# Two tiles of query features against the key-value sums at a time, in a fused attention and mixture-of-experts kernel

## The chip, the core and the metric

The kernel runs on one core of a Trainium2 chip. The metric is the device time of one execution in microseconds (us), the median of three runs. Engines are named as in the profile: PE (matrix multiplications; PEld are its weight loads), DVE (vector), ACT (activations), POOL (general purpose), SP (here it only issues DMAs).

## The reference

For 2048 tokens of width 512: layer norm, projections to queries, keys and values of 32 heads of 16, a feature map of each query and key (a small matrix per head, then two softmaxes of 16), and linear attention, whose numerator and denominator come from sums over all tokens.

```python
kv = jnp.einsum("bhsf,bhsd->bhfd", phi_k, v)
z  = jnp.einsum("bhsf->bhf", phi_k)
num = jnp.einsum("bhqf,bhfd->bhqd", phi_q, kv)
den = jnp.einsum("bhqf,bhf->bhq", phi_q, z)[..., None] + 1e-6
o = num / den
...
h = x + _A_ref(_layernorm(x, axis=-1), A_wqkv, A_w_phi, A_wo)
h2 = h + _B_ref(_layernorm(h, axis=-1), B_w_gate, B_w1, B_w2)
```

`_A_ref` ends with the output product `@ wo`. `_B_ref` sends each token to the one of eight experts with the largest logit; an expert is a product to 1792 columns, a silu, and a product back to 512.

## The kernel before

The 2048 tokens are 16 tiles of 128. The first 177 us make the projections, the sums over keys and values (`kvbd`, which holds each head's sums and its denominator column) and the turned query features `phT0` to `phT15`, one per tile. The change lies in the stage behind that, the **attention-output stage**, from 177 us to 257 us of the span. Behind it follow the experts, in pairs of tiles, until the end.

The stage is the loop `for c in range(NT + 8)` (L1034). For a tile it has these steps, each run at its own distance behind the loop's counter:

- `s_num(c)` (L511) starts a DMA of the input tile `xt` two tiles ahead, issues 32 small products `pn` (L523, weights of 128x64, 68 columns) into two PSUM banks, and lets DVE invert the denominators (L527 `den`) and multiply (L528 `o`).
- `s_ot(c-1)` turns `o` with four PE transposes `pto` (L480); ACT splits it into a high part `xh` (L84) and DVE into the rest `xl` (L87). In what follows `xh(c)` and `xl(c)` are those of tile c.
- `s_wo(c-2)` is the output product `po` (24 matmuls, L90 to L92, high and low parts of the weights `wohi`, `wolo`); DVE adds the input to give `hb` (L924, or L928 in halves) and the gate logits `lg`; ACT sums `hb` (L932) and sums its squares (L935), with the negative mean `hnm` (POOL, L934) between the two. Further POOL steps (L937 to L939) finish the layer norm.
- every second tile, for a pair of tiles, DVE picks the expert (`s_top`), POOL works out the gate (`s_gate`, L966 to L971) and SP writes the pair to `hbuf` in DRAM (L972); PE and DVE rank the tokens within their experts (`s_rank`, products `pl`; `s_inv`, products `acc`).
- after eight tiles `s_star` chooses the expert that will go first: product `pc` (L1011), then DVE steps to the register value `esti` (L1017). SP loads it (L276) and starts four DMAs of that expert's weights, `raw0` to `raw3` (L278). `s_first` finds which tokens go first (product `gp0`, L1028; DVE `gidx` and `sidx`, L1029 and L1030), and POOL gathers them into `xg0` (L168).
- from then on the weights are split: ACT makes `whi` out of `raw` in quarter pieces (L84), DVE makes `wlo` (L235). They stand on ACT and DVE between the last tiles' steps.

The stage ends with the turn `mtr` of the first gathered tokens (L197), the output product of tile 15, and the first expert's first product `mh` (256.76 us).

Each engine works through its own queue in order, and waits at the head of it for semaphores of the others. The order of a queue is made when the kernel is built, by a scheduler that follows the program's order and the `after(...)` constraints. PSUM has four banks that `pn`, `pto`, the tile's own `po` (tiles 0, 13 and 15), `mtr` and `mh` take in turn: who takes a bank waits until its last contents have been read. The other output products share one pair of banks. There are five buffers for `xt`.

Of the kernel before, what the change touches and what calls it, by code (L numbers as in the profile page):

```python
# [27 lines left out]
NT = S // P  # L28
# [27 lines left out]
def kernel(  # L56
# [20 lines left out]
    def bc(ap, n):  # L77
        return ap.unsqueeze(len(ap.shape)).to_broadcast(list(ap.shape) + [n])
# [29 lines left out]
    po, pol, isS, nS, mS, isP = [pos[:, i:i + 1] for i in range(6)]  # L108
# [38 lines left out]
    def after(i):  # L147
        return tc.issue_after(i.ins) if i is not None else ExitStack()

    def bank(name):  # L150
        return ps.tile([P, 512], F32, name=name, tag="b")
# [263 lines left out]
    with ExitStack() as actx:  # L415
# [40 lines left out]
        st = [dict() for _ in range(NT)]  # L456

        def row(name, bufs, tag):
            return work.tile([P, D], F32, name=name, tag=tag, bufs=bufs)

        def load_x(c, queue=nc.sync):
            st[c]["xt"] = row("xt", 5, "xt")
            queue.dma_start(st[c]["xt"], x[c * P:(c + 1) * P, :])
# [33 lines left out]
        def proj2(ab, whi, wlo, name, outer=False, own=False):  # L497
            pw = None
            if outer or own:
                p = [bank(name) for _ in range(2)]  # L500
            else:
                pw = psw.tile([P, 2, 512], F32, name=name, tag="w")
                p = [pw[:, i, :] for i in range(2)]
            for a in range(KD if outer else 2):
                for b in range(2 if outer else KD):
                    i, k = (b, a) if outer else (a, b)
                    m = mm3(p[i][:, 0:HC], ab[0][:, k, :], ab[1][:, k, :], whi[:, k, i, :], wlo[:, k, i, :],
                            k == 0, k == KD - 1)
            return p, m, pw

        def s_num(c):  # L511
            if c == 0:
                load_x(0)
                load_x(1)
            if c + 2 < NT:
                load_x(c + 2)
            o = row("o", 2, "pc").rearrange("p (h f) -> p h f", f=DH)
            for i in range(2):
                pn = bank("pn")
                for g in range(4):  # L520
                    for s in range(2):
                        r = slice(64 * s, 64 * s + 64)
                        st[c]["pn"] = T.matmul(pn[r, g * 68:(g + 1) * 68], phT[c][:, 4 * i + g, r],  # L523
                                               kvbd[:, 4 * i + g, :], start=True, stop=True)
                nv = pn[:, 0:272].rearrange("p (h f) -> p h f", f=DH + 1)
                den = work.tile([P, 16, 1], F32, name="den")
                V.reciprocal(den, nv[:, :, DH:DH + 1])  # L527
                st[c]["on"] = V.tensor_tensor(o[:, 16 * i:16 * i + 16, :], nv[:, :, 0:DH],  # L528
                                              den.to_broadcast([P, 16, DH]), op=OP.mult)
            st[c]["o"] = o.rearrange("p h f -> p (h f)")  # L530
# [5 lines left out]
        if True:  # L536
# [106 lines left out]
            def feat1(p, c, whole=True):  # L643
                pv = p.rearrange("p (h f) -> p h f", f=DH)
                mn = work.tile([P, H], F32, name="mn")
                V.tensor_reduce(mn, pv, AX.X, OP.min)
                t = wp.tile([P, H, 2, DH], F32, name="t", bufs=3)
                V.tensor_tensor(t[:, :, 1, :], bc(mn, DH), pv, op=OP.subtract)
                return feat1b(p, c, t) if whole else t

            def feat1b(p, c, t):
                pv = p.rearrange("p (h f) -> p h f", f=DH)
                mx = work.tile([P, H], F32, name="mx")
                V.tensor_reduce(mx, pv, AX.X, OP.max)
                pin["f1"] = V.tensor_tensor(t[:, :, 0, :], pv, bc(mx, DH), op=OP.subtract)  # L655
                pin["ex"] = A.activation(t, t, AF.Exp, scale=st[c]["rstd"])  # L656
                return t.rearrange("p h s f -> p (h s) f")
# [244 lines left out]
                    pin["kv"] = V.tensor_tensor(kvbd[r, :, 17 * h:17 * h + 17], kvps[0][r, :, k:k + 17], epsz[r], op=OP.add)  # L902
            with after(pin["kv"]):
                t15 = feat1(pq[2], NT - 1, False)
            s_num(0)
            s_num(1)
            s_ot(0)

# [2 lines left out]

        def s_wo(c):
            b, j = divmod(c, NB)
            with after(st[min(c + 2, NT - 1)]["pn"]):
                p, st[c]["po"], po = proj2(st[c]["oT"], wohi, wolo, "po", own=c in (0, NT - 3, NT - 1))
            if j == 0:
                bt[b]["hb"] = work.tile([P, NB * ROW], F32, name="hb", tag="ph", bufs=3).rearrange(
                    "p (j r) -> p j r", r=ROW)
                bt[b]["lg"] = work.tile([P, NB, E], F32, name="lg", bufs=3)
            h = bt[b]["hb"][:, j, :]  # L920
            hv, xv = h[:, 0:D].rearrange("p (i d) -> p i d", i=2), st[c]["xt"].rearrange("p (i d) -> p i d", i=2)
            lg = bt[b]["lg"][:, j, :].rearrange("p (i e) -> p i e", i=2)
            if po is not None:
                V.tensor_tensor(hv, po[:, :, 0:D // 2], xv, op=OP.add)  # L924
                st[c]["lg"] = V.tensor_tensor(lg, po[:, :, D // 2:HC], xwg[:, c], op=OP.add)
            else:
                for i in range(2):
                    V.tensor_tensor(hv[:, i, :], p[i][:, 0:D // 2], xv[:, i, :], op=OP.add)  # L928
                    st[c]["lg"] = V.tensor_tensor(lg[:, i, :], p[i][:, D // 2:HC], xwg[:, c, i, :], op=OP.add)
            junk = row("junk", 3, "xn")  # L930
            sm = work.tile([P, 2], F32, name="hsum")
            A.activation(junk, h[:, 0:D], AF.Copy, accum_out=sm[:, 0:1])  # L932
            nm = work.tile([P, 1], F32, name="hnm")
            G.tensor_scalar(nm, sm[:, 0:1], -1.0 / D, None, op0=OP.mult)  # L934
            st[c]["sq"] = A.activation(junk, h[:, 0:D], AF.Square, bias=nm, accum_out=sm[:, 1:2])  # L935
            ve = work.tile([P, 1], F32, name="ve")
            G.tensor_scalar(ve, sm[:, 1:2], 1.0 / D, EPS, op0=OP.mult, op1=OP.add)  # L937
            G.tensor_tensor(h[:, D + 1:D + 2], ve, nhalf, op=OP.pow)
            st[c]["hp"] = G.tensor_tensor(h[:, D:D + 1], nm, h[:, D + 1:D + 2], op=OP.mult)  # L939
# [65 lines left out]
        def at(fn, c, n=NT):  # L1005
            if 0 <= c < n:
                fn(c)
# [25 lines left out]
        LOS = {NT - 4: range(0, 2), NT - 3: range(2, 4), NT - 2: range(4, 6), NT - 1: range(6, 8)}  # L1033
        for c in range(NT + 8):  # L1034
            if c > 1:
                at(s_num, c)
                if c == NT - 3:
                    s_wo(c - 2)
                at(s_ot, c - 1)
# [16 lines left out]
            if c not in (NT - 3, NT + 1):  # L1056
                at(s_wo, c - 2)
            if c in (4, 6, 8):
                s_qt(NT - 3 + c // 2 - 2)
            if c == NT:  # L1060
                with after(st[NT - 2]["po"]), after(st[NT - 1]["oT"][2]), after(st[NT - 2]["lg"]):
                    x0 = xhi[0][:, :, 0:P], xlo[0][:, :, 0:P]
                    xl0 = turn(*x0)[1]
                with after(pin["mtr"]):
                    s_wo(NT - 1)
                with after(st[NT - 1]["hp"]):
                    s_gate(b)
# [602 lines left out]
```

## Time and profile before

| | us |
|---|---|
| median of 3 runs (lowest, highest) | 633.71 (633.68, 633.88) |
| the profiled execution's own time | 634.18 |
| its span | 632.4 |
| attention-output stage in the span | 177.1 to 256.8 |
| ACT, busy over the span | 373.3 |
| POOL, busy over the span | 246.6 |

Start times below are us from the span's start. A row of the timeline has the start, the busy time, the engine, the line and the operation, the tiles written and read, the shape, the count of equal instructions joined in the row, and in square brackets the idle time ahead of it with what ended it. The duration of a PE row has a modelled end, so that neighbouring rows overlap; PE's pace is read from the distance of starts. The profiled execution took 0.47 us longer than the median.

### The profile page before, as it was taken

The page shows a single profiled execution, that of the slowest core. Times are in us where ns is not written, and L with a number is a line of the kernel's source. Part 1 is how long each engine was busy: PE and PEld are TensorE (multiplying, and loading weights), DVE is VectorE, ACT ScalarE, POOL GpSimd, SP SyncE. Part 2 cuts the span into 40 slices and gives each one's busy share as a digit, 9 for nine tenths or more (in the row PEclk, how much of TensorE's full clock was granted, in tenths as well). Part 3 has the DMA queues.
Part 4 walks back from the last instruction along what each step waited for, and adds up shares of the span by engine and source line. Part 5 has one row for each costly group of instructions (what it writes and reads, how often), then busy time and mean ns, then how long its engine had stood idle before and what let it go on. Part 6 is the DMA issues. An engine that isn't in the chain of part 4 may idle for free. (4 is left out here: it accounts for less than half of the span.)

```text
span 632.4 us, 14731 instructions
## 1 busy us (share of the span) xinstructions
PE 622.4 (98%) x5455; PEld 555.0 (88%) x5455; DVE 452.2 (72%) x900; ACT 373.3 (59%) x673; POOL 246.6 (39%) x345
## 2 busy tenths in 40 slices
PE   8999999999999999999999999999999999999996
PEld 7888888888889999868998899999999889988884
DVE  7988786888898788966324666666555775579992
ACT  6666766577434449634325666566456666668781
POOL 5586778787616554521122221210401420023220
PEclk9999999999999999999999999999999999999998
DMA  8712111111002359249221586563755595569921
GB/s 315 253 36 61 42 51 52 51 52 35 18 20 85 118 205 380 85 160 399 78 72 43 170 299 206 208 235 135 267 174 206 180 336 170 195 217 372 421 83 36
DMA packets 25689, 103.09 MB, mean 163 GB/s; under 512 B 3422, under 2 KB 3422, under 8 KB 17536
## 3 DMA queue, kind: packets, MB, share of 16 engines
q1 hardware_dynamic: 21088, 88.15, 39.1%
q0 software_dynamic: 4368, 13.82, 6.5%
q8 instruction: 46, 0.75, 0.5%
q14 instruction: 43, 0.35, 0.2%
q10 hardware_dynamic: 144, 0.02, 0.0%
HBM read 93.56 MB, written 8.81 MB: 162 GB/s over the span
## 5 line engine op out<-in xcount | busy, mean ns | idle before, releaser
L235 DVE TENSOR_TENSOR wlo<-raw,whi 128x1024 fp32r<-128x1024 f32 (+1 forms) x133 | 152.0, 1166 | 27.2 <-ACT whi L84 24.9
L84 ACT ACTIVATE whi<-raw 128x1024 fp32r<-128x1024 f32 (+1 forms) x134 | 129.1, 998 | 1.5 <-DVE wlo L235 0.6
L168 POOL DMA_INDIRECT xg<-hbuf,gidx x34 | 43.4, 1275 | 134.2 <-DMA out_dram<-xg,sidx 34.1
L87 DVE TENSOR_TENSOR hA<-hs,hA 128x256 fp32r<-128x256 f32 (+1 forms) x84 | 36.6, 435 | 74.7 <-ACT hA L84 53.7
L664 POOL TENSOR_TENSOR ph<-t,sm 128x1024 f32<-128x1024 f32 x32 | 62.1, 1941 | 16.9 <-DVE sm L662 16.6
L90 PE MATMUL gw<-xhi,whi 128*128 128x256 f32 x224 | 64.1, 286 | 0.0
L91 PE MATMUL gw<-xlo,whi 128*128 128x256 f32 x224 | 63.0, 281 | 0.0
L92 PE MATMUL gw<-xhi,wlo 128*128 128x256 f32 x224 | 63.0, 281 | 0.0
L1419 ACT ACTIVATE hs<-gw 128x256 f32<-128x256 f32 x56 | 21.4, 382 | 63.2 <-PE gw L92 52.7
L661 DVE TENSOR_REDUCE sm<-t 128x64 f32<-128x1024 f32 x32 | 38.9, 1215 | 20.0 <-ACT t L656 17.9
L656 ACT ACTIVATE t<-t,rstd 128x1024 f32<-128x1024 f32 x32 | 36.8, 1151 | 27.2 <-DVE t L655 24.7
L181 POOL DMA_INDIRECT out_dram<-xg,sidx x17 | 19.9, 1173 | 78.1 <-DVE xg L1271 42.9
L90 PEld LDWEIGHTS gw<-xhi,whi 128*128 128x128 f32 x224 | 42.2, 188 | 1.7
L91 PEld LDWEIGHTS gw<-xlo,whi 128*128 128x128 f32 x224 | 42.3, 189 | 1.6
L92 PEld LDWEIGHTS gw<-xhi,wlo 128*128 128x128 f32 x224 | 42.2, 189 | 0.0
L90 PE MATMUL po<-wohi,xh 128*128 128x260 f32 x128 | 37.4, 293 | 0.1
L84 ACT ACTIVATE hA<-hs 128x256 fp32r<-128x256 f32 (+1 forms) x84 | 35.8, 427 | 2.6
L92 PE MATMUL po<-wohi,xl 128*128 128x260 f32 x128 | 36.6, 286 | 0.3 <-DVE xl L87 0.2
L91 PE MATMUL po<-wolo,xh 128*128 128x260 f32 x128 | 36.1, 282 | 0.0
L90 PE MATMUL pv<-wvhi,xh 128*128 128x260 f32 x120 | 34.1, 284 | 0.0
L92 PE MATMUL pv<-wvhi,xl 128*128 128x260 f32 x120 | 33.9, 282 | 0.0
L91 PE MATMUL pv<-wvlo,xh 128*128 128x260 f32 x120 | 33.9, 282 | 0.0
(425 smaller groups left out, 1919.9 us busy)
## 6 DMA issues: line engine op xcount, KB each, us to landing
raw<-in_w_dram SPq DMA_DIRECT2D x63, 1024.0 KB, 6.5
xt<-in_x_dram SPq DMA_DIRECT2D x32, 256.0 KB, 2.7
hbuf<-hb SPq DMA_DIRECT2D x8, 515.0 KB, 3.6
xT<-in_xTs_dram SPq DMA_DIRECT2D x16, 256.0 KB, 2.6
phT<-in_wv_dram SPq DMA_DIRECT2D x4, 256.0 KB, 4.4
phT<-in_wqkT_dram SPq DMA_DIRECT2D x4, 256.0 KB, 5.1
phT<-in_wqkT_dram SPq DMA_DIRECT2D x2, 512.0 KB, 6.3
phT<-in_wo_dram SPq DMA_DIRECT2D x2, 512.0 KB, 8.2
```

Of the source, the lines that this page charges most:

```text
L84: return A.activation(dst, src, AF.Copy)
L87: return V.tensor_tensor(dst, src, hi.bitcast(F32), op=OP.subtract)
L90: T.matmul(ps, ahi, bhi, start=first, stop=False)
L91: T.matmul(ps, ahi, blo, start=False, stop=False)
L92: return T.matmul(ps, alo, bhi, start=False, stop=last)
L168: G.indirect_dma_start(out=dst[0:n, :], out_offset=None, in_=hbuf if col else hbuf[0:S // 2, :], in_offset=bass.IndirectOffsetOnAxis(ap=gi ...
L181: m = G.indirect_dma_start(out=out, out_offset=bass.IndirectOffsetOnAxis(ap=sidx[0:n, col:col + 1], axis=0), in_=src[0:n, 0:D], in_offset= ...
L235: return eng.tensor_tensor(lo, r, h.bitcast(F32), op=OP.subtract)
L656: pin["ex"] = A.activation(t, t, AF.Exp, scale=st[c]["rstd"])
L661: V.tensor_reduce(sm, t, AX.X, OP.add)
L664: pin["f2"] = G.tensor_tensor(ph.rearrange("p (a f) -> p a f", f=DH), t, bc(sm, DH), op=OP.mult)
L1419: A.activation(h, p, AF.Silu)
```

## The change

`s_num` no longer starts the DMA of `xt`; the first four are started ahead of the loop and the others from the loop. In the loop `s_num` runs for two tiles, c and c+1, when c is even, and not at all when c is odd. The two are placed behind the output product of tile c-3. The output product of a tile, which had to come behind `pn` of the tile two further on, now has to come behind the `pn` of the pair that ends two or three further on. `s_ot` and `s_wo` are called tile by tile as before.

```diff
         def s_num(c):
-            if c == 0:
-                load_x(0)
-                load_x(1)
-            if c + 2 < NT:
-                load_x(c + 2)
             o = row("o", 2, "pc").rearrange("p (h f) -> p h f", f=DH)
...
+            for c in range(4):
+                load_x(c)
             s_num(0)
             s_num(1)
             s_ot(0)
...
         def s_wo(c):
             b, j = divmod(c, NB)
-            with after(st[min(c + 2, NT - 1)]["pn"]):
+            with after(st[min(c + 3 - c % 2, NT - 1)]["pn"]):
...
             if c > 1:
-                at(s_num, c)
+                if c + 2 < NT and c > 1:
+                    load_x(c + 2)
+                if c % 2 == 0 and c < NT:
+                    with after(st[c - 3]["po"] if c > 2 else None):
+                        s_num(c)
+                        s_num(c + 1)
                 if c == NT - 3:
                     s_wo(c - 2)
                 at(s_ot, c - 1)
```

Three lines fewer stand ahead of the stage's later steps, so a line of before from L924 on is three less in the changed kernel (L934 becomes L931), and L523 becomes L518. The rows below are the queues as built, with what each instruction waits for.

The first place is PE at tiles 14 and 15 (`phT14`, `phT15`). Before, `pn` of tile 14 is followed by the turn of tile 13 and the output product of tile 12 (`po_4076`):

```order
L523 MATMUL pn_4043<-kvbd_146,phT14_142 64x68 [waits DMAHW2_49]
L523 MATMUL pn_4043<-kvbd_146,phT14_142 64x68 x7
L523 MATMUL pn_4055<-kvbd_146,phT14_142 64x68 [waits DVE_49,PE_49]
L523 MATMUL pn_4055<-kvbd_146,phT14_142 64x68 x7
L480 MATMUL pto_4067<-ident_61,o_3937 128x128 [waits DVE_49,PE_49]
L480 MATMUL pto_4067<-ident_61,o_3937 128x128 x3
L90 MATMUL po_4076<-wohi_144,xh_4004 128x260 [waits DVE_49,Activation_49]
```

Now, with `po_4101` the output product of tile 12:

```order
L518 MATMUL pn_4043<-kvbd_146,phT14_142 64x68 [waits DMAHW2_49]
L518 MATMUL pn_4043<-kvbd_146,phT14_142 64x68 x7
L518 MATMUL pn_4055<-kvbd_146,phT14_142 64x68 x8
L518 MATMUL pn_4068<-kvbd_146,phT15_143 64x68 [waits DMAHW3_49]
L518 MATMUL pn_4068<-kvbd_146,phT15_143 64x68 x7
L518 MATMUL pn_4080<-kvbd_146,phT15_143 64x68 [waits DVE_49,PE_49]
L518 MATMUL pn_4080<-kvbd_146,phT15_143 64x68 x7
L90 MATMUL po_4101<-wohi_144,xh_4004 128x260 [waits PE_49,Activation_49]
```

The four banks are now taken by the four halves of two tiles in a row; the last half (`pn_4080`) takes the bank that the turn of tile 12 had, and waits until DVE has read it for `xl(12)`. The two DMA waits are for loads at the program's start into the same buffers.

The second place is the hand-over to the first expert, on ACT and POOL. On ACT, before (`hb_3883` holds tiles 10 and 11, `pto_3999` is the turn of tile 12):

```order
L932 ACTIVATE junk_3887,hsum_3888<-hb_3883 128x512 [waits DVE_49]
L935 ACTIVATE junk_3887,hsum_3888<-hb_3883,hnm_3890 128x512 [waits Pool_49]
L84 ACTIVATE whi0_3700<-raw0_3522 128x512 [waits DMAHW2_49]
L84 ACTIVATE whi0_3700<-raw0_3522 128x512 x3
L84 ACTIVATE xh_4004<-pto_3999 128x512 [waits PE_49]
L932 ACTIVATE junk_3989,hsum_3990<-hb_3883 128x512 [waits DVE_49]
L84 ACTIVATE whi1_3702<-raw1_3523 128x512 [waits DMAHW3_49]
```

and now (`hb_3908` holds tiles 10 and 11):

```order
L84 ACTIVATE xh_4004<-pto_3999 128x512 [waits PE_49]
L929 ACTIVATE junk_3912,hsum_3913<-hb_3908 128x512 [waits DVE_49]
L84 ACTIVATE whi1_3727<-raw1_3523 128x512 [waits DMAHW3_49]
L932 ACTIVATE junk_3912,hsum_3913<-hb_3908,hnm_3915 128x512 [waits Pool_49]
L84 ACTIVATE whi0_3725<-raw0_3522 128x512 [waits DMAHW2_49]
L84 ACTIVATE whi0_3725<-raw0_3522 128x512 x3
```

A first piece of `whi1`, which waits for the second weight load, has moved ahead of the squares of tile 10 and of all of `whi0`; `xh(12)` has moved ahead of the sum of tile 10. On POOL at the same place, before:

```order
L970 TENSOR_TENSOR nr_3920<-gt_3919,fixed_66 128x2 [waits Pool_49]
L971 TENSOR_TENSOR hb_3644<-gt_3919,nr_3920 128x2 [waits Pool_49]
L934 TENSOR_SCALAR hnm_3890<-hsum_3888 128x1 [waits Activation_49]
L168 DMA xg0_3708<-hbuf_60,gidx_94 128x515 [waits DMAHW5_49,DMAHW0_49,DVE_49]
L937 TENSOR_SCALAR ve_3893<-hsum_3888 128x1 [waits Activation_49]
```

and now:

```order
L967 TENSOR_TENSOR nr_3945<-gt_3944,fixed_66 128x2 [waits Pool_49]
L968 TENSOR_TENSOR hb_3669<-gt_3944,nr_3945 128x2 [waits Pool_49]
L168 DMA xg0_3733<-hbuf_60,gidx_94 128x515 [waits DMAHW5_49,DMAHW0_49,DVE_49]
L931 TENSOR_SCALAR hnm_3915<-hsum_3913 128x1 [waits Activation_49]
L934 TENSOR_SCALAR ve_3918<-hsum_3913 128x1 [waits Activation_49]
```

The gather of the first tokens has moved ahead of the mean of tile 10, for which ACT's squares of tile 10 wait.

The third place is DVE at the choice of the first expert. Before, the rest `xl(10)` stands inside that chain:

```order
L1015 SCALAR_TENSOR_TENSOR sc<-pc,sm_3686,desc_72 128x8 [waits DVE_49]
L87 TENSOR_TENSOR xl<-pto,xh 128x512 [waits Activation_49]
L1016 TENSOR_REDUCE sm_3686<-sc 128x1 [waits DVE_49]
L1017 TENSOR_SCALAR esti<-sm_3686 128x1 [waits DVE_49]
L1018 TENSOR_SCALAR est_103<-sm_3686 128x1
```

Now it stands ahead of the two counts (`cum7`, `cum8`) from which `pc` is made, and nothing stands inside:

```order
L1011 TENSOR_REDUCE sm_3711<-pc 128x1 [waits PE_49]
L1012 SCALAR_TENSOR_TENSOR sc<-pc,sm_3711,desc_72 128x8 [waits DVE_49]
L1013 TENSOR_REDUCE sm_3711<-sc 128x1 [waits DVE_49]
L1014 TENSOR_SCALAR esti<-sm_3711 128x1 [waits DVE_49]
L1015 TENSOR_SCALAR est_103<-sm_3711 128x1
```

What moved is `xl(10)`, out of the chain and to the place ahead of it; `xh(10)` on ACT has moved likewise, ahead of the sum and the squares of tile 8.

## The prediction

> **What bounds the kernel now.** I read the page first, then the windows of the stage, then what PE waits for.
>
> ```profile
> PE 622.4 (98%) x5455; PEld 555.0 (88%) x5455; DVE 452.2 (72%) x900; ACT 373.3 (59%) x673; POOL 246.6 (39%) x345
> ```
>
> PE is busy for 622.4 of 632.4 us. That is an average over stages, so I look at the stage of the change, in columns of busy time and (instructions):
>
> ```profile
> 200.00:230.00 30.00, 30.00 (x405) 28.94 (x402) 24.52 (x106) 14.08 (x34) 17.11 (x44) 1.00 0.34 107
> 230.00:240.00 10.00, 10.00 (x136) 9.53 (x132) 8.15 (x35) 5.88 (x14) 6.13 (x14) 1.00 0.88 340
> 240.00:250.00 10.00, 9.87 (x121) 9.14 (x115) 9.72 (x39) 9.03 (x21) 4.44 (x14) 1.00 1.02 363
> ```
>
> The columns are PE, PEld, DVE, ACT, POOL, clock, DMA share. To 240 us PE is the bound alone (ACT half idle). From 240 to 250 us, where the first expert's weights are split, DVE (9.72 of 10) and ACT (9.03) are nearly full as well: what comes late there finds no room. Behind the stage, PE waits for nothing to speak of. These are the only PE waits from 258 us to the end, by line, total, times and longest:
>
> ```profile
> PE mh L90 <- PEq L1573: 0.6, 1, 0.6
> PE my L91 <- DVEq L1182: 0.2, 1, 0.2
> ```
>
> So what PE gains or loses until `mh` (256.76 us) reaches the end, but for at most the 0.2 us for which it now waits on DVE.
>
> **What the merge removes.** PE's pace, by starts:
>
> ```profile
> 184.44 0.28 PE L91 MATMUL po<-wolo,xh 128*128 128x260 f32 x1
> 184.56 0.28 PE L92 MATMUL po<-wohi,xl 128*128 128x260 f32 x1
> 184.77 1.17 PE L523 MATMUL pn<-kvbd,phT 128*64 128x68 f32 x32
> 185.87 0.66 PE L480 MATMUL pto<-ident,o 128*128 128x128 f32 x4
> ...
> 177.09 2.12 PE L523 MATMUL pn<-kvbd,phT 128*64 128x68 f32 x64
> ...
> 238.65 0.28 PE L92 MATMUL po<-wohi,xl 128*128 128x260 f32 x1
> 238.77 0.60 PE L480 MATMUL pto<-ident,o 128*128 128x128 f32 x4
> ```
>
> Within `po` a step is 0.12 us; into `pn` it is 0.21 (184.56 to 184.77), and from there to the turn 1.10. So a tile's `pn` stands between `po` and the turn for 1.31. Of 64 products in one go (177.09, where the kernel has a merged pair already, tiles 0 and 1) the second 32 cost 2.12 - 1.17 = 0.95, and the turn that then follows `po` directly comes 0.12 behind it (238.65 to 238.77). A merge saves 1.31 - 0.95 - 0.12 = 0.24; I take 0.25, since the turn is also shorter there (0.60 for 0.66). Before tile 10 there are four merges (1.0 us), in all seven: **1.75 us** for PE alone.
>
> The Trainium skill has a rule against this, "TensorE: Matmul & The Clock Gate", section "Step-by-step: what each phase is for": weight loads are pulled ahead of matmuls in flight, so that "*next* tile's weights load while *this* tile's matmul runs". By it the step into `pn` would cost no more than the 0.12 inside `po` and the merge would save next to nothing, which gives rival 4's time; the 0.21 of the row speaks against it here. The page "TensorEngine Tiling (Array Packing)", section "Key Properties", states that a change of tiling mode drains TensorE, which would fit the 0.21 (`pn` has weights of 128*64, its neighbours 128*128).
>
> The input loads cost SP nothing new: five buffers are still used, each load stands ahead of the same sums or one write earlier, and no `hb` of before waits for one.
>
> **The choice of the first expert** comes earlier. The timeline of PE, DVE and SP there, and the DMA view of one load:
>
> ```profile
> 225.68 0.66 PE L480 MATMUL pto<-ident,o 128*128 128x128 f32 x4
> ...
> 226.42 0.18 PE L1011 MATMUL pc<-cum,ones 128*128 128x8 bf16 x1
> ...
> 227.06 0.22 DVE L1015 SCALAR_TENSOR_TENSOR sc<-pc,sm,desc 128x8 f32<-128x8 f32 x1
> 228.33 0.69 DVE L87 TENSOR_TENSOR xl<-pto,xh 128x512 fp32r<-128x512 f32 x1 [1.05 <-ACT xh L84]
> 228.93 0.15 DVE L1016 TENSOR_REDUCE sm<-sc 128x1 f32<-128x8 f32 x1
> 229.12 0.15 DVE L1017 TENSOR_SCALAR esti<-sm 128x1 int32<-128x1 f32 x1
> ...
> 230.90 0.34 SPq L278 DMA_DIRECT2D raw<-in_w_dram  x1
> ...
> raw<-in_w_dram SPq DMA_DIRECT2D x1, 1024.0 KB, 8.3
> ```
>
> `xl(10)` cost this chain 228.93 - 227.06 - 0.2 = 1.7. It now stands ahead of the counts: the turn of tile 10 comes about 1.0 earlier than its 225.68 of before, then 0.6 for `xh`, 0.6 for `xl`, 0.2 for two counts, so that `pc` can run at about 226.7. PE would reach it at 226.2 and loses 0.5 there. From `pc` it is 0.85 to `esti` without `xl`: 227.55, **1.57 earlier**. `raw1` (the second load; the last two rows are its issue and its time to landing) lands at 239.2 before, at 237.6 now. Of the gain, 0.8 is left to PE at tile 12 and 1.0 again at tile 14, where the sixth merge is made: `pn(14)` at 238.4 for 239.38.
>
> **The hand-over** takes more than that back. The timelines of POOL, ACT and DVE there:
>
> ```profile
> 236.45 0.20 POOL L971 TENSOR_TENSOR hb<-gt,nr 128x2 f32<-128x2 f32 x1
> 236.60 0.22 POOL L934 TENSOR_SCALAR hnm<-hsum 128x1 f32<-128x1 f32 x1
> 237.31 1.23 POOL L168 DMA_INDIRECT xg<-hbuf,gidx  x1 [0.48 <-DVE o L528]
> ...
> 236.86 0.72 ACT L935 ACTIVATE junk<-hb,hnm 128x512 f32<-128x512 f32 x1 [1.21 <-POOL hnm L934]
> 237.49 0.19 ACT L935 ACTIVATION_READ_ACCUMULATOR junk<-hb,hnm 128x1 f32 x1
> 237.58 2.17 ACT L84 ACTIVATE whi<-raw 128x512 fp32r<-128x512 f32 x4
> 239.66 0.57 ACT L84 ACTIVATE xh<-pto 128x512 fp32r<-128x512 f32 x1
> ...
> 238.23 1.30 DVE L235 TENSOR_TENSOR wlo<-raw,whi 128x512 fp32r<-128x512 f32 x2 [1.27 <-ACT whi L84]
> 239.44 0.69 DVE L924 TENSOR_TENSOR hb<-po,xt 128x512 f32<-128x512 f32 x1
> 240.04 0.16 DVE L925 TENSOR_TENSOR lg<-po,xwg 128x8 f32<-128x8 f32 x1
> ```
>
> The chain of before is `hnm(10)` on POOL, squares of tile 10 on ACT, `whi0`, `wlo0` on DVE, and behind `wlo0` in DVE's queue `hb(11)` and `xl(12)`. Two things now stand in its way. POOL makes the gather ahead of `hnm(10)`: the gate of tiles 8 and 9, now at 236.65, ends about 0.6 earlier, at 236.0 (not the whole 1.0: DVE's part of it stands behind `xl(11)`, and the turn of tile 11 now comes behind two `pn`); then 0.4 as in the row, 1.23 for the gather, 0.22 for `hnm(10)`: 237.9. And ACT takes a piece of `whi1` first: `raw1` at 237.6 and 0.55 for a piece (2.17 / 4) give 238.2. The two nearly agree; the later one counts. The squares start at 238.2 for 236.86, `whi0` at 238.9, `wlo0` 0.65 behind (237.58 to 238.23) at 239.55, `hb(11)` 1.2 later at 240.75, `xl(12)` 0.7 later at 241.45 (the half of `wlo0` that stood between them is behind now), and it is read out at about 242.1.
>
> That matters since the last half of `pn(15)` takes the bank of the turn of tile 12. PE is there at 238.4 + 3 x 0.47 = 239.8 and **waits 2.3 us**. Before, this bank is taken far behind `xl(12)`, and the wait isn't there.
>
> The end of the stage, on PE, ACT and DVE:
>
> ```profile
> 239.38 1.17 PE L523 MATMUL pn<-kvbd,phT 128*64 128x68 f32 x32
> ...
> 252.43 0.57 ACT L84 ACTIVATE xh<-pto 128x512 fp32r<-128x512 f32 x1
> 253.06 0.38 PE L90 MATMUL po<-wohi,xh 128*128 128x260 f32 x1
> 253.78 0.39 PE L92 MATMUL po<-wohi,xl 128*128 128x260 f32 x1 [0.22 <-DVE xl L87]
> 254.84 0.68 DVE L924 TENSOR_TENSOR hb<-po,xt 128x512 f32<-128x512 f32 x1
> 256.76 0.47 PE L90 MATMUL mh<-whi,xhi 128*128 128x512 f32 x1
> ```
>
> From `pn(14)` (239.38) to `mh` PE needs 17.38 us, less the wait of 0.22 and the seventh merge's 0.25: 16.9. From 238.4 that is 255.3, with the wait 257.6. `po(15)` starts 3.7 ahead of it, at 253.9, and after four matmuls wants `xl(15)`. ACT reaches `xh(15)` 14.85 behind `whi0` (237.58 to 252.43), now 0.7 more for squares that stand ahead of it and 1.0 less for what is done already: 253.5. On DVE `hb(14)` (254.84 before) now stands ahead of `xl(15)`; it starts when `po(14)` ends, at 253.7, and 0.6 each for both, and 0.15, free PE at 255.05 where it would go on at 254.4: 0.6 more. `mh` comes at about 258.2, **1.4 later**. At most 0.2 is won back behind (above). The sum is -1.75 of merges, +0.5 at `pc`, +2.3 at `pn(15)`, +0.4 at `po(15)` (0.6 for 0.22), -0.2 behind: 1.2 against the profiled 634.18, less its 0.47 over the median: **634.9 us**. The unknown is what POOL and ACT do at the hand-over: 0.7 either way.
>
> **Rivals.**
>
> 1. The hand-over keeps its slack. The 1.27 of DVE and the 1.21 of ACT ahead of `wlo0` and the squares are idle time in the rows, and if the gather frees POOL early (its busy time on POOL is rough) nothing binds. Then the 1.75 arrives whole: 634.18 - 1.75 - 0.47 = **632.0**. Against it: the DVE queue holds `xl(12)` behind `wlo0` whatever POOL does, and 1.27 is less than the 2.3 wanted.
> 2. The tail gives back just the saving. If POOL's gate moves with PE by 1.0 and `raw1` is there in time, all of the hand-over stands 1 us earlier than I reckon, and PE's wait is 1.3: **633.9**, from 633.3 to 634.3.
> 3. Slower, and clearly: `raw1` lands no earlier than before, at 239.2. Then the `whi1` piece ends at 239.7, the squares start 1.5 later than I reckon, and all behind moves with them: **636.4**. It decides once `raw1` lands later than about 237.4. For it: `esti` hangs on a count that only follows `xl(10)`. Against it: nothing of before stands between `esti` and the loads but SP's register load.
> 4. The change of weight shape costs nothing, or costs the same in merged pairs; the step of 0.21 is then something else. The saving goes, the hand-over's end (set by POOL and ACT) stays where it is: **635.2**.
>
> **How the numbers follow.** The forecast has 0.45, rival 1 0.2, rival 2 0.15, rival 3 0.15, rival 4 0.05. A measurement of this kernel can tell 0.2% from no change, 1.27 us: faster means under 632.44, slower over 634.98. Faster is rival 1 alone, 0.2. The forecast (634.2 to 635.6) is cut by the upper bound, 0.25 below and 0.2 above; with rival 2 and a little of rival 4 below, rival 3 and the rest of rival 4 above, no change has 0.41 and slower 0.39. The range of 8 in 10 goes from rival 1's value to just over rival 3's, 632.0 to 636.4, which leaves out half of each.
>
> **What would show it.** In the profile after: rows of `pn` with 64 products at every second tile, and the turn of tile 10 about 1.0 ahead of 225.68 (else rival 4); `esti` near 227.5 and `raw1` landed near 237.6 (else rival 3); the squares of tile 10 near 238.2, with idle time in front ended by POOL's `hnm` or by `raw1`; a PE wait of about 2.3 us on `xl(12)` in `pn`, near 240; `mh` near 258.2. If `pn(15)` has no wait and `mh` comes ahead of 256, rival 1 holds. Wrong in any case would be a new wait behind 262 us, of which the rows of before show no sign.

## The result, and the profile after

| | us |
|---|---|
| before, timed in turn with it: median of 5 (lowest, highest) | 633.88 (633.68, 635.1) |
| changed: median of 5 (lowest, highest) | 642.32 (641.77, 644.02) |
| ratio, 95% interval | 1.0129 (1.0117 to 1.014) |
| the changed kernel's profiled execution | 641.77 |
| its span, beside 632.4 before | 640.1 |

The change costs 8.4 us. The page of the changed kernel, and its windows of the stage (columns as before: PE, PEld, DVE, ACT, POOL, clock, DMA share, GB/s):

```profile
span 640.1 us, 14739 instructions
PE 623.3 (97%) x5455; PEld 556.2 (87%) x5455; DVE 453.0 (71%) x900; ACT 373.8 (58%) x673; POOL 248.4 (39%) x345
```

```profile
200.00:230.00 30.00, 27.24 (x376) 26.05 (x374) 22.78 (x91) 13.44 (x32) 16.79 (x42) 1.00 0.30 90
230.00:240.00 10.00, 9.53 (x128) 9.12 (x129) 8.65 (x43) 4.25 (x11) 4.88 (x15) 1.00 0.73 255
240.00:250.00 10.00, 7.40 (x103) 7.15 (x104) 5.74 (x23) 7.81 (x19) 4.94 (x12) 0.92 1.02 384
```

The engines do the same work, but PE now stands idle: 2.8 us between 200 and 230, where it had been full, and 2.6 between 240 and 250, where the granted clock is also below 1. What PE waited for from 177 to 262 us (line, releaser, total, times, longest):

```profile
PE pn L518 <- DVE xl L87: 2.6, 1, 2.6
PE po L90 <- DVE lg L922: 2.0, 3, 1.1
PE po L90 <- DVE cum L952: 1.5, 1, 1.5
PE pto L480 <- DVE o L523: 0.8, 1, 0.8
PE po L90 <- ACT xh L84: 0.6, 1, 0.6
PE po L90 <- DVE oh L948: 0.4, 1, 0.4
```

Before there was one wait of 0.2. The first row was forecast, at 2.3. Rows two, three and six were not: there a whole output product `po` stands still at its first matmul until DVE has done something with the output product before it (`lg` is the last read of `po`; `cum` and `oh` stand just behind it in DVE's queue, and the view puts two of the waits down to them). The first of these waits, on PE and then on DVE:

```profile
195.43 0.60 PE L480 MATMUL pto<-ident,o 128*128 128x128 f32 x4
197.50 0.36 PE L90 MATMUL po<-wohi,xh 128*128 128x260 f32 x1 [1.48 <-DVE cum L952]
```

```profile
194.94 1.21 DVE L656 TENSOR_REDUCE sm<-t 128x64 f32<-128x1024 f32 x1
196.07 0.15 DVE L952 TENSOR_TENSOR cum<-cum,oh 128x8 bf16<-128x8 bf16 x1
196.19 0.55 DVE L657 RECIPROCAL sm<-sm 128x64 f32<-128x64 f32 x1
196.66 0.63 DVE L921 TENSOR_TENSOR hb<-po,xt 128x512 f32<-128x512 f32 x1
197.20 0.15 DVE L922 TENSOR_TENSOR lg<-po,xwg 128x8 f32<-128x8 f32 x1
197.27 0.15 DVE L952 TENSOR_TENSOR cum<-cum,oh 128x8 bf16<-128x8 bf16 x1
```

From the turn to the product it is 2.07 us, where 0.41 were enough before (from the turn at 185.87):

```profile
186.28 0.37 PE L90 MATMUL po<-wohi,xh 128*128 128x260 f32 x1
```

Two products now follow each other with little more than a turn between them, both in the one shared pair of banks. DVE empties it late here because its own queue has 1.8 us of a feature map's sums (L656 and L657, 1.21 and 0.55) ahead of `hb`. Behind the middle, `pn(14)` starts at 243.29, 3.9 later than before, though six merges had been made; `mh` at 264.94, 8.2 later.

### The profile page after: what moved, and what is told of

Its sections match the earlier page's. It is cut to its first block, busy times and chain, and to the rows that moved or that the text cites. A ratio compares the mean times of both kernels' runs of the same rounds, so it can differ in the third digit from the quotient of the medians.

```text
span 640.1 us, 14739 instructions
## 1 busy us (share of the span) xinstructions
PE 623.3 (97%) x5455; PEld 556.2 (87%) x5455; DVE 453.0 (71%) x900; ACT 373.8 (58%) x673; POOL 248.4 (39%) x345
## 5 line engine op out<-in xcount | busy, mean ns | idle before, releaser
L168 POOL DMA_INDIRECT xg<-hbuf,gidx x34 | 44.7, 1313 | 131.3 <-DMA out_dram<-xg,sidx 32.3
L659 POOL TENSOR_TENSOR ph<-t,sm 128x1024 f32<-128x1024 f32 x32 | 62.1, 1939 | 19.3 <-DVE sm L657 15.4
L656 DVE TENSOR_REDUCE sm<-t 128x64 f32<-128x1024 f32 x32 | 38.9, 1215 | 19.9 <-ACT t L651 17.8
```

Of the source, the lines that this page charges most:

```text
L168: G.indirect_dma_start(out=dst[0:n, :], out_offset=None, in_=hbuf if col else hbuf[0:S // 2, :], in_offset=bass.IndirectOffsetOnAxis(ap=gi ...
L656: V.tensor_reduce(sm, t, AX.X, OP.add)
L659: pin["f2"] = G.tensor_tensor(ph.rearrange("p (a f) -> p a f", f=DH), t, bc(sm, DH), op=OP.mult)
```

## Experiments

All kernels are the changed one with the edit shown, timed in turn with the kernel before on the same chip. There were four such groups, so times of different groups are compared by their ratios. The median of before was 634.38 beside `own_banks`, `tail_single`, `tail_merged` and `loads_only`; 634.76 beside `fix_act`, `fix_pool`, `fill` and `own_tail`; 634.80 beside `own_12`, `own_14` and `fill_half`; and 634.70 beside `own_12_cum`. The edits are parts of the code; `...` stands for what is left out.

**Where the loss lies.** Three runs divide the change: banks of their own for the odd output products (`own_banks`), and each half of the loop changed alone (`tail_single`, `tail_merged`). A fourth (`loads_only`) changes only the place of the input loads. The first:

```diff
-p, st[c]["po"], po = proj2(st[c]["oT"], wohi, wolo, "po", own=c in (0, NT - 3, NT - 1))
+p, st[c]["po"], po = proj2(st[c]["oT"], wohi, wolo, "po", own=c % 2 == 1 or c == 0)
```

> The output products of all odd tiles get two of the four rotating banks instead of the shared pair. Theory (the second product of a pair waits until DVE has read the first one out of the shared pair): the five waits ahead of odd products, 1.7, 1.4, 0.7, 0.7 and 0.6 us in the changed kernel's trace, shrink to 0.1 or less; up to 0.5 us a pair comes back where pn then waits for these banks; 637 to 639.5 us. Rival (these products wait for their own inputs, xh and xl, from ACT and DVE): the waits stay and the time is 642 to 643.

Measured 634.39 us, ratio 0.9995 (0.9986 to 1.0004): the whole loss is gone, more than either side expected. PE's waits from 177 to 267 us:

```profile
PE pn L518 <- DVE xl L87: 1.4, 2, 0.9
PE po L90 <- DVE jm L989: 0.5, 1, 0.5
PE pn L518 <- PE pn L518: 0.4, 1, 0.4
```

No product waits for `lg`, `cum` or `oh` any more: the shared pair was the cause of those waits. The wait of `pn(15)` shrank too, to 0.5 on `xl(12)` and 0.4 on PE itself (the 0.9 is at tile 6, the 0.5 of `po` at tile 15). The reason stands in the queues: with this edit the scheduler again puts POOL's gather behind `hnm(10)` and ACT's `whi0` ahead of `whi1`. So this run alone does not separate the middle from the hand-over; the next two do. In both, the `after` of the output products in `s_wo` is made to fit the tiles that are paired. Pairs up to tile 11 only:

```diff
...
-if c % 2 == 0 and c < NT:
+if c % 2 == 0 and c < 12:
...
+elif c >= 12:
+    at(s_num, c)
```

> Pairs up to tiles 10 and 11, tile by tile from tile 12 on. Theory (the stage's middle and the hand-over lose on their own): the middle keeps its loss of about 4 us, the 2.6 us wait of pn(15) and the lower clock behind it go, the hand-over of before returns: 637 to 638.5 us. Rival (the hand-over suffers only because the middle is late): the wait shows again elsewhere, 640 or more.

Measured 638.20 us, 1.0052 (1.0038 to 1.0066), as expected. The complement, pairs only from tile 12 on:

```diff
...
+if c < 12:
+    at(s_num, c)
-if c % 2 == 0 and c < NT:
+elif c % 2 == 0 and c < NT:
...
```

> Tile by tile up to tile 11, pairs for 12, 13 and 14, 15: the other half of the change. Theory: no waits ahead of odd products until tile 11, but pn(15) waits for xl(12) by 2 to 3.5 us near 241 us and the granted clock falls behind it; 637 to 639 us. Rival (the hand-over suffers only because the middle is late): 634 us.

Measured 638.58 us, 1.0065 (1.0051 to 1.0079), as expected. Up to tile 10 the middle is that of before, and the hand-over shows the forecast wait:

```profile
PE pn L518 <- DVE xl L87: 2.7, 1, 2.7
PE po L90 <- ACT xh L84: 0.6, 1, 0.6
PE po L90 <- DVE lg L922: 0.4, 1, 0.4
```

The last row is a wait for the shared banks, at output product 11, whose `pn` the pair of tiles 12 and 13 took away. By the medians, the pairs up to tile 11 cost 3.8 us and the other two 4.2: together 8.0 of the 8.4 of the change. The hand-over is not late because the middle is late.

> Only the place in the program from which the input loads are started is changed; sums are tile by tile as before. All theories: as before, 633.5 to 634.3 us. If it is more than 1 us slower, the loads and not the pairs are the cause.

Measured 634.22 us, 0.9999 (0.999 to 1.0008): the loads cost nothing.

**Which order makes the hand-over late.** The changed kernel's rows there, on POOL, ACT, DVE and PE:

```profile
241.88 1.23 POOL L168 DMA_INDIRECT xg<-hbuf,gidx  x1 [0.67 <-issue]
243.14 0.27 POOL L931 TENSOR_SCALAR hnm<-hsum 128x1 f32<-128x1 f32 x1
...
242.87 0.63 ACT L84 ACTIVATE whi<-raw 128x512 fp32r<-128x512 f32 x1 [2.09 <-DMA raw<-in_w_dram]
243.45 0.72 ACT L932 ACTIVATE junk<-hb,hnm 128x512 f32<-128x512 f32 x1
...
244.82 1.29 DVE L235 TENSOR_TENSOR wlo<-raw,whi 128x512 fp32r<-128x512 f32 x2 [3.79 <-ACT whi L84]
246.70 0.68 DVE L87 TENSOR_TENSOR xl<-pto,xh 128x512 fp32r<-128x512 f32 x1
...
243.29 1.64 PE L518 MATMUL pn<-kvbd,phT 128*64 128x68 f32 x48
247.53 0.66 PE L518 MATMUL pn<-kvbd,phT 128*64 128x68 f32 x15 [2.60 <-DVE xl L87]
```

The chain is the one of the prediction: the squares of tile 10 (243.45), `whi0`, `wlo0`, `xl(12)`, `pn(15)`. Both causes end within 0.05 us of each other, POOL's `hnm(10)` at 243.41 and ACT's piece of `whi1` at about 243.45. One run (`fix_act`) holds ACT's pieces of `whi1` behind the squares of tile 10:

```diff
-with ..., after(xn0 if c == NT - 1 else None):
+with ..., after(st[c - 3]["sq"] if c == NT - 3 else xn0 if c == NT - 1 else None):
```

> The changed kernel, with ACT's pieces of whi1 held behind the squares of tile 10; POOL still makes the gather ahead of hnm(10). In the changed kernel's trace hnm(10) ended at 243.41 and the whi1 piece at 243.45, so each alone holds the squares. Theory (either is enough): the wait of pn(15) stays at 2.6 less at most 0.5 us, 641 to 643 us. Rival (ACT's order alone is the cause): the wait shrinks by 2 us, 638.5 to 639.5.

Measured 641.68 us, 1.0108 (1.0089 to 1.0126). The squares now wait for POOL, `pn(15)` waits 2.6 as in the changed kernel, and the span is 640.3 beside 640.1:

```profile
243.70 0.72 ACT L932 ACTIVATE junk<-hb,hnm 128x512 f32<-128x512 f32 x1 [2.67 <-POOL hnm L931]
```

The other (`fix_pool`) holds the gather behind `hnm(10)` (`nm`):

```diff
-G.tensor_scalar(nm, ...)
+st[c]["nm"] = G.tensor_scalar(nm, ...)
...
-rows(xg[0], 0)
+with after(st[10]["nm"]):
+    rows(xg[0], 0)
```

> The changed kernel, with the gather held behind hnm(10) on POOL, which puts ACT's whi1 behind the squares of tile 10 as well. Theory (these two orders make the hand-over late): the squares of tile 10 start about 2 us earlier (near 241.5), the wait of pn(15) falls from 2.6 to under 1 us, the granted clock stays full, 638 to 639.5 us; the waits ahead of odd products stay. Rival (the hand-over is late because the output products before it are): no less than 641.

Measured 638.55 us, 1.0061 (1.0047 to 1.0075), as expected. ACT's squares start 0.65 us after it is free, and PE waits 0.60 instead of 2.60, although its middle is as late as in the changed kernel (`pn(14)` starts at 243.95):

```profile
242.11 0.72 ACT L932 ACTIVATE junk<-hb,hnm 128x512 f32<-128x512 f32 x1 [0.65 <-POOL hnm L931]
```

```profile
246.19 0.69 PE L518 MATMUL pn<-kvbd,phT 128*64 128x68 f32 x16 [0.60 <-DVE xl L87]
```

So POOL's order alone is enough to make the hand-over late, and ACT's is not its only cause. A kernel with POOL's order put right and ACT's left as it is was not run, so that ACT's order alone would be enough is read from the rows and not shown.

**What the wait does to the clock.** The windows of the changed kernel behind the wait, and two steps of output product 12 there:

```profile
248.00:250.00 2.00, 2.00 (x17) 1.93 (x13) 2.00 (x12) 1.91 (x5) 0.91 (x4) 0.60 1.13 416
250.00:252.00 2.00, 2.00 (x13) 2.00 (x11) 0.95 (x5) 0.46 (x1) 0.39 (x1) 0.55 1.00 370
```

```profile
250.94 0.42 PE L91 MATMUL po<-wolo,xh 128*128 128x260 f32 x1
251.16 0.42 PE L92 MATMUL po<-wohi,xl 128*128 128x260 f32 x1
```

A step is 0.22 us where it had been 0.12, at a granted clock of 0.55 to 0.60. The 15 matmuls ahead of the turn took 3.2 us (248.15 to 251.38) for 1.9, and the turn behind them 0.57 (to 251.95) for 0.35: 1.5 us in all. To test that it is the idle time, PE gets work in the wait, in `s_num` ahead of the last half of tile 15 (`fill`):

```diff
+if c == NT - 1 and i == 1:
+    fill = pss.tile([P, 512], F32, name="fill", tag="s")
+    for _ in range(20):
+        T.matmul(fill[:, 0:P], ident, ident, start=True, stop=True)
```

> The changed kernel, with 20 products of 128x128 on PE ahead of the last half of pn(15), into a PSUM buffer that nobody reads: about 2.2 us of work in the 2.6 us in which PE waits there. Theory (the idle time makes the granted clock fall to 0.55 to 0.60 for the 4 us behind it, which cost 1.3 us): the clock stays at 1.00 and output product 12 keeps a step of 0.12; 640.5 to 641.5 us. Rival (the slow steps behind the wait come from something else): the step of 0.21 stays and the time is 642 to 643.

Measured 642.13 us, 1.0119 (1.0102 to 1.0136). The time missed, since a product ran as two passes: 40 of them, 4.5 us, longer than the wait. The clock was at 1.00 in every window and the step at 0.12. With ten products, the tenth in a second buffer (`fill_half`):

> The changed kernel with 10 products in the wait of pn(15) (they ran as two passes of 0.114 us each in the run fill, so 2.3 us in all, less than the wait of 2.6). Theory (idle time lets the granted clock fall): clock 1.00 from 240 to 257 us, output product 12 at a step of 0.12, and 640.5 to 641.5 us. Rival: the step of 0.21 stays, 642 to 643.

Measured 641.61 us, 1.0108 (1.0093 to 1.0122), above the 640.5 to 641.5 expected (the kernel before took 0.9 longer beside this run, 634.80, than beside the changed kernel, 633.88). The windows are at full clock:

```profile
248.00:250.00 2.00, 2.00 (x26) 1.87 (x27) 2.00 (x12) 2.00 (x5) 1.06 (x3) 1.00 1.11 400
250.00:252.00 2.00, 2.00 (x19) 2.00 (x18) 2.00 (x7) 1.78 (x4) 0.18 (x1) 1.00 0.98 396
```

So the idle time makes the clock fall. In the trace `mh` comes at 263.89, 1.05 earlier than in the changed kernel. The filling was not free: its last product stood behind the end of the wait and took 0.42 (247.49 to 247.91), and the scheduler made another order of the products behind it. So the price of the clock is taken from the steps above, 1.5 us, and not from this time. `fix_pool` agrees with it: from `pn(14)` to `mh` it takes 18.34 us for 21.65 in the changed kernel (243.95 to 262.29; 243.29 to 264.94). Of these 3.3 the shorter wait is 2.0; the rest is the clock's 1.5, less 0.2 by which `po(15)` waits longer there.

**Is there a better version?** With own banks in the middle and the tail tile by tile, the merges' gain should be left over.

The first try (`own_tail`) is the edit of `tail_single` and

```diff
-p, st[c]["po"], po = proj2(..., own=c in (0, NT - 3, NT - 1))
+p, st[c]["po"], po = proj2(..., own=c in (0, 3, 5, 7, 9, 11, 13, 15))
```

> Pairs up to tiles 10 and 11 with banks of their own for the odd output products, tile by tile from tile 12 on as before. Theory: five merges gain 0.3 us each, the waits of pn on its banks (1.2 and 0.25 us in the run with own banks) take most of it back, the hand-over is that of before: 633.4 to 634.4 us beside 634.0 to 634.4 for the kernel before. Rival (own banks cost DVE two more instructions a tile, and that shows): 634.5 to 635.5.

Measured 637.95 us, 1.0043 (1.0026 to 1.006): a miss on both sides. The next (`own_12`) has the edits of `tail_single` and of `own_banks`, so that it differs from `own_tail` in tile 1 alone; the one behind it (`own_14`) keeps tiles 12 and 13 in a pair as well:

> As the run with own banks, but tiles 12 to 15 one by one. Against the run own_tail only tile 1's output product differs (own banks here). Theory (own_tail lost about 4 us in its middle because two DVE additions stood 1.8 us behind POOL's long multiplication and xh(6) came late on ACT, which the banks of tile 1 shift): 633 to 634.5 us. Rival (the tail from tile 12 on apart costs that much whatever the banks): 637 to 638.5.

> Own banks for the odd output products, pairs up to tiles 12 and 13, tiles 14 and 15 one by one as before. Theory: the run with own banks (same time as the kernel before) still had waits of pn(15) on xl(12), 1.2 us, and of output product 15, 0.75 us; with tiles 14 and 15 apart both go, so 632.3 to 633.3 us, faster than before by 0.2%. Rival (as in the run with own banks and the tail from tile 12 on apart, 638: the middle's order of ACT and POOL beside it decides): 636 or more.

`own_12` measured 634.20 us, 0.9994 (0.9983 to 1.0005), as expected; `own_14` 634.68, 0.9996 (0.9987 to 1.0004), between what its two sides expected. `own_12` differs from `tail_single` (1.0052) in the banks alone, with the hand-over of before in both: this is the plainest measure of what the shared pair cost in the middle. But who has which bank at tile 1 decides about 4 us as well: in `own_tail` `hnm(2)` stands on POOL behind a long multiplication (L659) that itself waits, ACT waits ahead of the squares that need it, and `xh(5)` behind them comes late (the squares, and `xh(5)`, on ACT):

```profile
203.57 0.72 ACT L932 ACTIVATE junk<-hb,hnm 128x512 f32<-128x512 f32 x1 [5.09 <-POOL hnm L931]
...
206.51 0.58 ACT L84 ACTIVATE xh<-pto 128x512 fp32r<-128x512 f32 x1
```

PE waits 1.9 for the `xl(5)` made of it, and soon after 1.5 for `cum`, which stands on DVE for as long as POOL's next multiplication runs. Behind these two waits the granted clock is low as well:

```profile
214.00:216.00 2.00, 2.00 (x39) 1.87 (x34) 2.00 (x15) 1.52 (x4) 0.93 (x3) 0.50 0.41 120
216.00:218.00 2.00, 2.00 (x12) 2.00 (x13) 1.59 (x7) 0.61 (x2) 1.08 (x3) 0.65 0.07 24
```

That was read from its trace and not tried by itself. `own_14` did lose the waits of `pn(15)`, but gained nothing on `own_12`: by the starts, 1.2 and 0.25 lost at tiles 6 and 8 and 0.47 at a turn take back what six merges give. The wait at tile 6 in `own_12`, on DVE and on POOL:

```profile
198.19 1.99 DVE L952 TENSOR_TENSOR cum<-cum,oh 128x8 bf16<-128x8 bf16 x2
200.11 0.68 DVE L87 TENSOR_TENSOR xl<-pto,xh 128x512 fp32r<-128x512 f32 x1
```

```profile
198.23 1.94 POOL L659 TENSOR_TENSOR ph<-t,sm 128x1024 f32<-128x1024 f32 x1
```

These are two additions of eight columns, 0.15 us each elsewhere. The second took 1.8 and ends when POOL's multiplication ends, and `xl`, for which `pn` waits, stands behind it. Moved to POOL (`own_12_cum`):

```diff
-bt[b]["cum"] = V.tensor_tensor(cum[c + 1], cum[c], oh[:, j, :], op=OP.add)
+bt[b]["cum"] = (G if b < 2 else V).tensor_tensor(cum[c + 1], cum[c], oh[:, j, :], op=OP.add)
```

> As own_12, with the four additions cum of the first two pairs on POOL instead of DVE. Theory (in the runs with own banks DVE stood at such an addition for 1.8 us, for as long as POOL's long multiplication ran, and xl behind it made pn wait 0.9 us for its bank): DVE isn't held there, the waits of pn at tile 6 (1.15 us) and tile 8 (0.25 us) go, 632.5 to 633.5 us, faster than before by 0.2%. Rival (pn waits there for another reason, or another DVE instruction is held in the same way): 634 us or more, with the wait still in the trace.

Measured 634.25 us, 0.9993 (0.9983 to 1.0003), slower than expected. DVE is not held and `pn` does not wait, but the ranking product `pl` now waits for `cum`, behind the same multiplication:

```profile
PE pl L977 <- POOL cum L952: 1.4, 2, 1.1
```

The wait changed its place. None of the versions is measurably faster than the kernel before.

## Why the prediction was wrong, point by point

- **The merge** was priced a little low: it saves more than was forecast. Two rows each of PE, at the starts of `pn(10)` and `pn(12)`, before and in `own_12_cum`, where PE doesn't wait between them (the views are narrow, so that a count is not that of the whole `pn`):

```profile
219.88 0.28 PE L523 MATMUL pn<-kvbd,phT 128*64 128x68 f32 x2
229.38 0.34 PE L523 MATMUL pn<-kvbd,phT 128*64 128x68 f32 x4
```

```profile
220.75 0.34 PE L518 MATMUL pn<-kvbd,phT 128*64 128x68 f32 x4
229.95 0.28 PE L518 MATMUL pn<-kvbd,phT 128*64 128x68 f32 x2
```

  9.50 and 9.20: 0.30 a merge for the 0.25 taken. The first merge, tiles 2 and 3, saved only 0.17 (from `pn(2)` to `pn(4)` 8.96 in the changed kernel for 9.13), so it is about 2.0 in all and not 1.75. Rival 4 falls. In the trace of before the first weight load of `pn` starts with its product, both at 184.77, and not beside the product ahead of it. The rule that weights are loaded beside running matmuls ("TensorE: Matmul & The Clock Gate" in the Trainium skill, section "Step-by-step: what each phase is for") would have left next to nothing of the saving; the runs disagree with it here.
- **The step that failed** is "What the merge removes": it priced what goes away between `po` and the turn, and not what had been covered by it. Before, `pn` and the turn (1.5 us) stood between two output products in the same pair of banks, and DVE read the first in that time. The merge takes `pn` away from every second place. It is a wait that takes the place of the time removed, and no rival named it. Five such waits cost 5.2 us (from the turn's start to the product's 2.07, 1.74, 1.05, 1.09 and 0.98, less 0.35 each for the turn itself), and one of 0.9 at a turn came with them. Less 1.7 of six merges and some 0.4 for `gp0`, which no longer interrupts a `pn`, that is within 0.1 of the 3.9 by which `pn(14)` is late. Own banks take all five away.
- **The choice of the first expert** did not come earlier. On PE and DVE of the changed kernel:

```profile
229.01 0.61 PE L480 MATMUL pto<-ident,o 128*128 128x128 f32 x4
231.52 0.18 PE L1008 MATMUL pc<-cum,ones 128*128 128x8 bf16 x1
...
232.40 0.15 DVE L1014 TENSOR_SCALAR esti<-sm 128x1 int32<-128x1 f32 x1
```

  `esti` is 3.4 us behind the turn of tile 10 in both kernels (225.68 and 229.12 before). The turn itself is 3.3 later for the waits ahead. Taking `xl(10)` out of the chain gained nothing: from `pc` to `esti` it is 0.9 for 2.7, about as forecast, but `pc`, now behind `xl(10)`, runs 2.5 behind the turn for 0.7 (2.0 forecast). PE did not lose the 0.5 at `pc`. The second weight load came late with `esti`: ACT's wait for it ended at 242.87, where 239.2 is rival 3's time. What rival 3 feared thus came, but from the waits ahead, and `pn(14)` was about as late.
- **The hand-over** was right in mechanism and nearly in size: 2.6 for 2.3, by the two orders that were named, which were forecast to agree within 0.3 and did within 0.05. `fix_pool` and `fix_act` show it for POOL's order. So rivals 1 and 2, by which the hand-over keeps its slack or is 1 us less late, fall as well.
- **The clock** was missing: the sum took the wait at its length, and the slow stretch behind it cost 1.5 us more. With it the hand-over comes to 2.6 + 1.5 + 0.4 (next point) less 0.3 for the seventh merge, 4.2, beside the 4.3 by which the way from `pn(14)` to `mh` grew (21.65 for 17.38).
- **`po(15)`** waited 0.65 for `xh(15)` where 0.6 for `xl(15)` was forecast; 0.22 of it was there before, so the term is 0.4 as in the sum. That the size fits although PE waited for ACT's `xh(15)` and not for `xl(15)` is luck.
- **Behind the stage** 0.5 was won back, 0.2 forecast (`mh` is 8.2 later, the span 7.7 longer).

The terms now: -2.0 of merges, +5.2, +0.9 and -0.4 in the middle, +2.6, +1.5 and +0.4 in the hand-over, -0.5 behind: 7.7, as in the spans.

## What to carry to other kernels

Before a gap on the busiest engine is closed, ask who worked in it: here a buffer was emptied in just the time that looked like overhead. With one shared buffer, two producers must stay as far apart as its reader needs, and the reader's queue is part of that distance. Where a scheduler makes the order, a change in one place moves instructions elsewhere; the queues as built showed the hand-over's wait ahead of the result, and would probably have shown the other had every pair of users of one buffer been gone through. A wait on the busiest engine can cost more than its length, here 2.6 us and 1.5 more of slow matmuls behind it.

## What the runs showed of the hardware

- PE idle for 2.6 to 2.7 us brought the granted clock down to 0.50 to 0.60 for up to 4 us behind it (the changed kernel, `tail_merged`). A single wait of 1.5 us in the changed kernel did not, but two of 1.9 and 1.5 within 7 us did (`own_tail`: 0.50 and 0.65 in the two windows behind them). Work in the same place kept it at 1.00 (`fill`, `fill_half`). The Trainium skill, "TensorE: Matmul & The Clock Gate", section "What's actually happening", states that the clock is halved after an idle window of about 3.4 us. The runs agree in kind; here a shorter wait was enough.
- A DVE addition with both inputs in SBUF was held for as long as a POOL multiplication ran, 1.8 us for 0.15 (`own_12`). The Trainium skill, "GPSIMD Engine Reference", section "Specifications", names it: the SBUF interfaces are shared, with contention for DVE instructions with two SBUF inputs, or in a 2-port performance mode. The additions agree with the first. In the changed kernel an operation of two columns (L983) took 1.06 us for 0.11 and ended with POOL's multiplication in the same way, and the turn that waited 0.8 us for `o` stood behind it. It has one tensor input; in which mode it ran no run shows.
